# Clustered attention and two MLP layers on one core: inverse sums spread by transposes, a mask transposed by pairs of tiles, the first MLP weights decoded in a written order

## The chip, the core and the metric

The kernel runs on one core of one Trainium2 chip. The metric is device time in microseconds (us), from the start of the program to its end; before the change it is 804.18 us, the median of three runs. The engines are named as the profile names them: PE (TensorE; its weight loads are PEld), DVE (VectorE), ACT (ScalarE), POOL (GpSimd) and SP (SyncE, which issues the DMAs). Each takes its instructions in the order of its own queue, and waits for others by semaphores.

## What is computed

Attention over 2 batches of 8 heads, 768 rows, head size 64, in which a query sees only the keys of its own cluster of 16; the result is the input of two MLP layers one after the other (512 to 2048 to 512, on 1536 tokens).

```python
    q_assign = np.argmax(np.einsum('bhsd,hcd->bhsc', q_n, c_n), axis=-1)
    k_assign = np.argmax(np.einsum('bhsd,hcd->bhsc', k_n, c_n), axis=-1)
    mask = q_assign[:, :, :, None] == k_assign[:, :, None, :]
    scores = scale * np.matmul(q, k.transpose(0, 1, 3, 2))
    scores = np.where(mask, scores, -1000000000.0)
    scores = scores - np.max(scores, axis=-1, keepdims=True)
    attn = np.exp(scores)
    attn = attn / (np.sum(attn, axis=-1, keepdims=True) + 1e-09)
    return np.matmul(attn, v).astype(np.float32)
...
    h = np.maximum(x @ w_in, 0.0)
    return (h * h @ w_out).astype(np.float32)
...
    h = x @ w_in
    relu6 = np.clip(h + 3.0, 0.0, 6.0)
    g = h * relu6 / 6.0
    return (g @ w_out).astype(np.float32)
```

Here `q_n`, `k_n` and `c_n` are the rows of q, k and the centroids divided by their norms. The inputs come as 64-bit floats in HBM: the weights are read as pairs of 32-bit words and put together on the chip ("decoding").

## The kernel before

**Precision.** Every fp32 operand of a product is split in two parts (`H` and `L`, `eh` and `el`, `gh` and `gl`, `xh` and `xl`, `hi` and `lo` of `w`) that PE multiplies at its faster rate; a product is then two or three matmuls.

**Attention, to about 278 us.** A unit is two heads of one batch: 8 units, each of 12 tiles of 128 queries, 96 tiles in all. A tile `n` goes through these steps: four matmuls `s` (L650 the products, L653 with the 16 mask rows behind a part of the operand `op`), the row maximum on DVE (L659), the exponential and its row sum on ACT (L670), two groups of three transposes on PE (L686), the split into `eh` and `el`, and the matmuls with the values (L713, four in a tile). The split is done by ACT and DVE, or, for the places in the set `ON_POOL` (11 of the 24 in a unit), by a copy `et` to SBUF and two POOL operations (L178, L694). `schedule` writes the order out by hand: each tile has five slots, and the tables `STEPS`, `FIRST`, `WEIGHTS`, `EARLY` and `AV` name the tile, relative to a unit's first, and the slot at which each other step of the unit is put: loads of the next unit's q, k and v, their transposes `tq` (L401), 12 stacking DMAs of 192 KB into `op`, cluster similarities, the mask, and after the unit the normalisation. POOL, DVE, ACT and PE get their instructions in that order; SP the DMAs.

**The mask.** `onehot` makes `oh`, 128 rows by 6 tiles by 64 columns (4 heads' worth of cluster flags for q and k). `mask` transposes each of the six on PE into one PSUM tile `toh` (L511), and one ACT operation over 64 partitions and 768 columns scales it into `mt` (L516), which four small DMAs (L524) bring into the rows 64 to 80 of `op`.

**The normalisation.** The 12 row sums of a unit are inverted on DVE into `ri`, 128 queries by 12. `emit_rows` transposes `ri` (`tr`, L742), splits it in `rh` (ACT, L745) and `rl` (DVE, L746), and sends the parts with four DMAs (L750) into four spare partitions, 96 to 99, of the next unit's `op` tile. `emit_norm` spreads them over 128 partitions by one matmul with a matrix `spread` of ones (`tn`, L759, twice a unit), multiplies the unnormalised result `U_t` by it on DVE, and splits into `XH`, `XL` on POOL. The last unit has no next `op` tile: there ACT writes a copy `rb` of `ri`, each value 64 times (L767), and three transposes of 128 by 128 (L769) bring it into place.

**The MLP, from about 278 us.** `decode` turns a chunk of weights (128 by 512 values, 512 KB in HBM) into `hi` and `lo` by seven steps: a clamp on POOL (`t`, L191), a scaling on ACT (`u`, L196), three integer operations on DVE (L201, L203, L208), a rounding on ACT (`hi`, L212) and a difference on DVE (`lo`, L214). Four chunks make one block of `w_in` or `w_out`. The first block of `w_in` is decoded in halves during the attention (`WEIGHTS`), as are the first 384 tokens' hidden values (`emit_early`). `mm1` makes the hidden values of a group of tokens, 4 `fb` of 12 matmuls, each `fb` followed by `gate` (ACT, ACT, POOL, DVE); `mm2` multiplies them by a block of `w_out`, 4 `db` of 12 matmuls, each with all four chunks. For the first block the tokens go in four groups of 384, after that in three of 512. This stage isn't written out by hand: a scheduler orders it from the program, whose loop asks for `mm1` of the groups 1 and 2, then `mm2` of 0 and 1, and so on, and whose tiles `t`, `u` and `a` of the decoding (`wd`) have one buffer each.

Of the kernel before, what the change touches and what calls it, by code (L numbers as in the profile page):

```python
# [23 lines left out]
    "load q": (-19, 0),  # L24
    "load k": (-24, 2),
    "load v": (-12, 4),
    "q0": (-15, 3),
    "q1": (-14, 1),
    "k0": (-14, 3),
    "k1": (-12, 0),  # L30
    "stack0": (-8, 3),
    "sim0": (-12, 4),
    "sim1": (-10, 0),
    "assign": (-10, 4),
    "stack1": (-6, 2),
    "leader": (-10, 4),
    "onehot": (-6, 2),
    "mask": (-5, 4),
    "v0": (-5, 2),
    "v1": (-3, 4),  # L40
    "rinv": (11, 0),
    "rows": (12, 2),
    "norm0": (16, 1),
    "norm1": (17, 0),
# [5 lines left out]
        "second1": (0, 3),  # L50
        "mask": (2, 1),
        "v0": (1, 3),
        "v1": (2, 3),
# [3 lines left out]
        "load v": (-7, 1),  # L57
        "k0": (-12, 1),
        "k1": (-10, 2),
        "stack0": (-10, 2),  # L60
        "sim0": (-9, 4),
        "sim1": (-7, 2),
        "assign": (-6, 2),
        "stack1": (-9, 0),
        "leader": (-6, 2),
        "onehot": (-5, 2),
        "mask": (-4, 3),
        "v0": (-2, 3),
        "v1": (0, 0),
    },  # L70
    2: {
        "load q": (-18, 4),
        "load k": (-17, 1),
        "load v": (-10, 3),
# [5 lines left out]
WEIGHTS = ((0, 2), (3, 4), (4, 4), (6, 0), (6, 3), (7, 3), (9, 3), (10, 0))  # L80
WEIGHTS_7 = (
    ((-1, 3), (0, 0), (0, 4), (1, 1), (1, 3), (1, 4), (2, 0), (2, 0)),
    ((2, 0), (4, 4), (5, 0), (5, 0), (5, 2), (5, 4), (6, 2), (7, 2)),
# [6 lines left out]
    ((2, 1), (2, 4), (3, 1)),  # L90
    ((5, 3), (5, 4), (6, 1)),
    ((7, 1), (7, 4), (9, 0)),
    ((9, 1), (10, 1), (10, 4)),
)

AV = ((3, 3), (3, 4), (4, 4), (5, 0), (5, 2), (5, 2))
# [3 lines left out]
    (0, 0), (1, 0), (1, 1), (2, 1), (4, 0), (4, 1), (6, 0), (7, 0), (9, 0), (9, 1), (11, 1),  # L100
# [5 lines left out]
    (0, 0), (2, 0), (4, 0), (5, 0), (6, 1), (8, 0), (8, 1), (9, 0), (10, 0),  # L106
# [4 lines left out]
    (2, 0), (5, 0), (6, 1), (10, 0),  # L111
# [6 lines left out]
E_U = "v"  # L118
# [3 lines left out]
E_XL = "p"  # L122
BIG = float(2**60)
# [5 lines left out]
def cluster_attention_mlp_kernel(  # L129
# [50 lines left out]
    def decode(pool, hi, lo, r, on_dve, clamp_on_dve=False):  # L180
# [7 lines left out]
        t = pool.tile(sh, F32, tag="t", name="t")  # L188
        u = pool.tile(sh, F32, tag="u", name="u")
        a = pool.tile(sh, I32, tag="a", name="a")  # L190
# [6 lines left out]
        else:  # L197
            nc.vector.tensor_scalar(u, t, 2.0**-112, None, op0=ALU.mult)
        yield
        ui = u.bitcast(I32)  # L200
        nc.vector.tensor_scalar(a, ui, 3, None, op0=ALU.logical_shift_left)  # L201
# [5 lines left out]
        v = t.bitcast(I32)  # L207
        nc.vector.scalar_tensor_tensor(  # L208
            v, ui, -0x80000000, a, op0=ALU.bitwise_and, op1=ALU.bitwise_or
# [40 lines left out]
    with ExitStack() as actx:  # L250
# [5 lines left out]
        msc = ac.tile([64, 1], F32, name="msc")  # L256
        mbi = ac.tile([64, 1], F32, name="mbi")
        nc.vector.memset(msc[0:32], 1.0)
        nc.vector.memset(msc[32:64], BIG)
        nc.vector.memset(mbi[0:32], 0.0)  # L260
        nc.vector.memset(mbi[32:64], -BIG)
        C = ac.tile([P, NJ, 160], F32R, name="c")
        C0 = ac.tile([P, 160], F32R, name="c0")
        spread = ac.tile([P, P], F32R, name="spread")[96:100]
# [76 lines left out]
        def centroid_prep(c):  # L341
# [4 lines left out]
            ones = sm_p.tile([P, HS], F32, tag="xx", name="ones")[96:100, :P]  # L346
            ones = ones.rearrange("p (i d) -> p i d", i=2)
            nc.gpsimd.memset(ones, 1.0)
            for base, sign in ((0, 1), (1, -1)):
                nc.gpsimd.affine_select(  # L350
                    ones, ones, pattern=[[-2 * sign, 2], [0, D]], compare_op=ALU.is_ge, fill=0.0,
                    base=base, channel_multiplier=sign,
                )
# [3 lines left out]
            nc.vector.tensor_copy(spread, ones.rearrange("p i d -> p (i d)"))  # L357
# [19 lines left out]
        def prep(u):  # L377
# [129 lines left out]
            def mask(r0=0, r1=R):  # L507
# [6 lines left out]
                if r0 == 0:  # L514
                    st["m"] = pr_p.tile([64, S], F32, tag="sim", name="mt", bufs=1)
                nc.scalar.activation(  # L516
                    st["m"].bitcast(F32R)[0:64, r0 * P : r1 * P], t[0:64, :n], AF.Identity,
                    scale=msc, bias=mbi,
                )
# [76 lines left out]
            def second_head(n):  # L596
# [27 lines left out]
                "rows": lambda: emit_rows(u),  # L624
# [112 lines left out]
        def emit_rows(u):  # L737

            if u == NU - 1:
                return  # L740
            t = ps_t.tile([P, 512], F32, tag="t", name="tr")
            nc.tensor.transpose(t[0 : 2 * R, :P], rinv[u], ident)  # L742
            rh = sm_p.tile([2 * R, P], F32R, tag="rh", name="rh", bufs=1)
            rl = sm_p.tile([2 * R, P], F32R, tag="rl", name="rl", bufs=1)
            nc.scalar.activation(rh, t[0 : 2 * R, :P], AF.Copy)  # L745
            nc.vector.tensor_sub(rl, t[0 : 2 * R, :P], f(rh))  # L746
            rows[u] = oper[u + 1][1][96:100, 1]
# [122 lines left out]
    with ExitStack() as mctx:  # L870
# [96 lines left out]
        for s, (m, fq, c, n) in enumerate(steps):  # L967
# [7 lines left out]
            if s:  # L975
                mm1(m, fq, c, n)
# [39 lines left out]
```

## Time and profile before

| | us |
|---|---|
| three runs | 801.37, 804.18, 806.17 |
| the profiled execution, its own time | 805.96 |
| its span (first to last instruction) | 804.3 |
| PE busy | 784.9 (98%) |
| DVE busy | 531.7 (66%) |
| ACT busy | 396.6 (49%) |
| POOL busy | 324.9 (40%) |
| mean granted clock of PE | 0.995 |

Busy is time in which an engine works on an instruction; matmuls overlap, so that a busy PE may still advance at less than its pace. For PE the time from one row's start to the next row's start tells more than a row's duration. A row on a stretch gives the busy times of PE, PEld, DVE, ACT and POOL in this order. A timeline row is: start, duration, engine, line, operation, output and inputs with their shapes, how many follow one another, and in brackets how long the engine had been idle before and what ended that.

### The profile page before, as it was taken

The numbers are of one execution on the slowest core, as the hardware profiler recorded it, in microseconds if no ns is written. First come the engines' busy times: TensorE is split into PE (matmuls) and PEld (weight loads), VectorE is DVE, ScalarE is ACT, GpSimd is POOL, SyncE is SP. The second block draws the span as 40 slices with busy tenths as digits, with TensorE's granted clock in tenths as the row PEclk, the third lists the DMA queues.
The fourth block names the chain that finished last, engine by engine and source line by source line (L and its number), as shares of the span: only waits on it lengthen the run. The fifth ranks groups of instructions, "written<-read, shape, count | busy, mean of one in ns | idle before, by whom it ended". The sixth has DMA issues, their size and how long they took to land.

```text
span 804.3 us, 11576 instructions
## 1 busy us (share of the span) xinstructions
PE 784.9 (98%) x4069; PEld 676.4 (84%) x4069; DVE 531.7 (66%) x897; ACT 396.6 (49%) x794; POOL 324.9 (40%) x441
## 2 busy tenths in 40 slices
PE   7989999999999989999999999999999999999998
PEld 6878998888888879988888888888888888888887
DVE  6879889888898574666666456586555665733432
ACT  5888898888886554554434334332343232211110
POOL 1759788778794551222322222333222222211110
PEclk9999999999999998999999999999999999999999
DMA  8838539448332023333222122121221211000012
GB/s 178 173 72 188 123 80 200 107 96 189 95 93 67 1 81 103 105 105 99 85 78 88 45 78 66 40 84 48 79 79 52 79 53 52 27 1 1 13 52 93
DMA packets 58537, 67.35 MB, mean 84 GB/s; under 512 B 41320, under 2 KB 41744, under 8 KB 58480
## 3 DMA queue, kind: packets, MB, share of 16 engines
q1 hardware_dynamic: 58480, 66.62, 31.2%
q8 instruction: 32, 0.52, 0.3%
q14 instruction: 25, 0.20, 0.1%
HBM read 43.02 MB, written 3.15 MB: 57 GB/s over the span
## 4 chain that ended last, share of the span: by engine, by line
PE 82%; DVE 4%; DMA 4%; ACT 3%; POOL 3%; issue 2%; SPq 2%; ACTq 0%; DVEq 0%; POOLq 0%
PE o L937 33%; PE h L231 30%; PE a L713 6%; PE t L686 5%; DMA op<-HL 3%; PE s L650 3%; PE s L653 2%; PE tsim L446 1%; SPq L298 1%; DVE nm L659 1%; POOL el L694 1%; ACT et L175 1%; DVE el L697 1%; DMA op<-mt 1%; PE tq L401 1%
## 5 line engine op out<-in xcount | busy, mean ns | idle before, releaser
L231 PE MATMUL h<-xh,w 128*128 128x512 f32 (+1 forms) x800 | 245.3, 382 | 0.5 <-ACT et L175 0.5
L231 PEld LDWEIGHTS h<-xh,w 128*128 128x128 f32 x800 | 149.3, 188 | 27.0 <-ACT et L175 0.7
L231 PE MATMUL h<-xl,w 128*128 128x512 f32 (+1 forms) x400 | 152.3, 381 | 0.0
L178 POOL TENSOR_SCALAR gh<-g 128x512 fp32r<-128x512 f32 (+1 forms) x96 | 70.5, 734 | 193.9 <-DVE g L242 133.5
L937 PE MATMUL o<-w,gh 128*128 128x512 f32 (+1 forms) x392 | 120.4, 385 | 0.0
L937 PE MATMUL o<-gh,w 128*128 128x512 f32 (+1 forms) x384 | 115.2, 376 | 0.0
L191 POOL TENSOR_SCALAR t<-wr 128x512 f32<-128x512 f32 (+1 forms) x66 | 46.4, 703 | 163.4 <-DVE w L214 162.2
L212 ACT ACTIVATE w<-t 128x512 fp32r<-128x512 f32 (+1 forms) x68 | 41.3, 607 | 127.3 <-DVE t L208 89.3
L244 DVE TENSOR_TENSOR gl<-g,gh 128x512 fp32r<-128x512 f32 (+1 forms) x96 | 65.2, 680 | 54.5 <-POOL gh L178 54.5
L686 PE MATMUL t<-ident,e 128*128 128x128 f32 x576 | 93.7, 275 | 4.5 <-ACT e L670 3.6
L659 DVE TENSOR_REDUCE nm<-s 128x1 f32<-128x768 f32 x96 | 91.0, 948 | 5.5 <-PE s L653 4.7
L694 POOL TENSOR_TENSOR el<-et,eh 128x384 fp32r<-128x384 f32 x86 | 89.1, 1036 | 7.2
L670 ACT ACTIVATE e<-s,nm 128x768 f32<-128x768 f32 x96 | 86.4, 900 | 3.0 <-DVE nm L659 2.7
L231 PEld LDWEIGHTS h<-xl,w 128*128 128x128 f32 x400 | 75.1, 188 | 13.0
L686 PEld LDWEIGHTS t<-ident,e 128*128 128x128 f32 x576 | 70.4, 140 | 17.9 <-ACT e L670 7.2
L937 PEld LDWEIGHTS o<-w,gh 128*128 128x128 f32 x392 | 73.1, 188 | 14.6
L937 PEld LDWEIGHTS o<-gh,w 128*128 128x128 f32 x384 | 71.4, 188 | 11.6 <-issue 0.3
L241 ACT ACTIVATE r<-h,three 128x512 f32<-128x512 f32 x48 | 32.5, 682 | 90.2 <-PE h L231 90.2
L196 ACT ACTIVATE u<-t 128x512 f32<-128x512 f32 (+1 forms) x62 | 38.7, 625 | 77.5 <-POOL t L191 76.5
L937 PE MATMUL o<-w,gl 128*128 128x512 f32 (+1 forms) x196 | 75.4, 385 | 0.0
L713 PE MATMUL a<-eh,vs 128*128 128x384 f32 x192 | 71.2, 371 | 1.2 <-DVE u L727 1.2
L937 PE MATMUL o<-gl,w 128*128 128x512 f32 (+1 forms) x192 | 72.1, 376 | 0.0
(127 smaller groups left out, 1273.8 us busy)
## 6 DMA issues: line engine op xcount, KB each, us to landing
wr<-in_moe_w_out_dram SPq DMA_DIRECT2D x32, 512.0 KB
op<-HL SPq DMA_DIRECT2D x84, 192.0 KB
wr<-in_moe_w_in_dram SPq DMA_DIRECT2D x28, 512.0 KB
rawv<-in_v_dram SPq DMA_DIRECT2D x16, 192.0 KB
out_dram<-acc SPq DMA_DIRECT2D x11, 256.0 KB
rawq<-in_q_dram SPq DMA_DIRECT2D x14, 192.0 KB
rawk<-in_k_dram SPq DMA_DIRECT2D x14, 192.0 KB
wr<-in_moe_w_in_dram SPq DMA_DIRECT2D x8, 256.0 KB
```

Source lines behind the costliest of these rows:

```text
L178: nc.gpsimd.tensor_scalar(dst, src, 1.0, 0.0, op0=ALU.mult, op1=ALU.add)
L191: (nc.vector if clamp_on_dve or not on_dve and E_CLAMP == "v" else nc.gpsimd).tensor_scalar(t, f(hw), MOST, -MOST, op0=ALU.min, op1=ALU.max)
L196: nc.scalar.activation(u, t, AF.Copy, scale=2.0**-112)
L212: nc.scalar.activation(hi, t, AF.Copy)
L231: nc.tensor.matmul(h, w[:, d, fs], x[:, d, cs], start=(d == 0 and n == 0), stop=(d == ND - 1 and n == 2),)
L244: nc.vector.tensor_sub(gl, g, f(gh))
L659: nc.vector.tensor_reduce(nm, S_t[n][:, :, :HS], axis=AX.XY, op=ALU.max, negate=True)
L670: nc.scalar.activation(e, s[:, :, :HS], AF.Exp, bias=nm, accum_out=sums[u][:, i * R + r : i * R + r + 1])
L686: nc.tensor.transpose(t[:, c, :], E_t[n][:, half, c * P : (c + 1) * P], ident)
L694: nc.gpsimd.tensor_sub(el, et, f(eh))
L713: nc.tensor.matmul(a[:, :HS], vs[:, kr, i, :], x[:, kr, :], start=(kr == 0 and x is eh), stop=(kr == R - 1 and x is el),)
L937: nc.tensor.matmul(o, lhsT, rhs, start=(k == 0), stop=(k == 3 * NF - 1))
```

## The change

- **Normalisation.** `emit_rows`, its transpose, its two operations and its four DMAs go, and so does `spread`. For every unit a copy `rb` (128 by 384, each inverse 64 times) is made twice, on POOL for the first seven units, on ACT for the last, at two new slots `spread0` and `spread1`; `emit_norm` transposes it in three pieces for all units.
- **Mask.** Two tiles of `oh` (128 columns) go through one transpose: three in place of six; the result lies in two halves of the partitions, so ACT scales it with two operations of 64 by 384.
- **Decoding.** The tile `a` goes, the integer steps work in `u` and `t`. In the weights decoded during the attention, `u` is made on ACT in place of DVE.
- **Begin of the MLP.** `mm1` of groups 1, 2 and 3 and `mm2` of groups 0, 1 and 2 are written out by hand, with the steps of the eight chunks of the next two blocks put between them by `decoding`; `t` has three buffers, `u` two; group 3's hidden values have a pool of their own. The weight pools are taken before the others, so their first buffers lie where the attention's tiles lay.
- **Slots.** Nearly all numbers of the tables are new; `ON_POOL` has ten places in place of eleven, `ON_POOL_LAST` ten in place of nine.

```diff
-    "mask": (-5, 4),
+    "mask": (-6, 3),
...
     "rinv": (11, 0),
-    "rows": (12, 2),
-    "norm0": (16, 1),
+    "rinv": (11, 3),
+    "spread0": (13, 1),
+    "spread1": (14, 1),
...
-E_U = "v"
+E_U = "a"
+E_RB = "p"
...
-        a = pool.tile(sh, I32, tag="a", name="a")
...
-                n = (r1 - r0) * P
-                for r in range(r0, r1):
+                for c in range(3):
                     nc.tensor.transpose(
-                        t[0:64, (r - r0) * P : (r - r0 + 1) * P], st["oh"][:, r, :], identb
+                        t[:, c * P : (c + 1) * P],
+                        st["oh"][:, 2 * c : 2 * c + 2, :].rearrange("p r c -> p (r c)"), identb,
                     )
...
+                for h in range(2):
+                    rs = slice(64 * h, 64 * h + 64)
+                    nc.scalar.activation(
+                        m[:, h], t[rs, : 3 * P].rearrange("p (c q) -> p c q", q=P), AF.Identity,
+                        scale=msc[rs], bias=mbi[rs],
+                    )
...
-        def emit_rows(u):
...
-            nc.tensor.transpose(t[0 : 2 * R, :P], rinv[u], ident)
...
-            nc.scalar.activation(rh, t[0 : 2 * R, :P], AF.Copy)
-            nc.vector.tensor_sub(rl, t[0 : 2 * R, :P], f(rh))
...
-                    nc.sync.dma_start(
-                        f(rows[u])[2 * i + x : 2 * i + x + 1, :],
...
+        def emit_spread(u, half):
...
+            rb = sm_p.tile([P, HS], F32, tag="rb", name="rb")
...
+            src = rinv[u].rearrange("p (i h r) -> p h r i", i=2, h=2)[:, half]
+            src = src.unsqueeze(3).to_broadcast([P, 3, 2, D])
+            if E_RB == "a" or u == NU - 1:
+                nc.scalar.activation(rb, src, AF.Copy)
+            else:
+                nc.gpsimd.tensor_copy(rb, src)
...
-                nc.tensor.matmul(
-                    t[:, :HS], spread, rows[u][:, half * HS : half * HS + HS], start=True, stop=True
+            for c in range(3):
+                nc.tensor.transpose(
+                    t[:, c * P : (c + 1) * P], rb[:, c].rearrange("p i d -> p (i d)"), ident
                 )
...
+        wd_p = mctx.enter_context(tc.tile_pool(name="wd", bufs=2, reuse_waits="tile"))
-        wd_p = mctx.enter_context(tc.tile_pool(name="wd", bufs=1, reuse_waits="tile"))
...
+        with tc.manual_schedule():
+            chunks = load_w(0, 0, 1) + load_w(0, 1, 0)
+            pieces = [2]
+            run(chunks[0], 2)
...
+            def decoding(after):
...
+                c, odd = divmod(pieces[0], 2)
+                pieces[0] += after
+                for when, chunk, n in (
+                    ((0, 0), c - 1, 3), ((0, 1), c - 2, 1), ((0, 1), c, 1),
+                    ((1, 1), c - 2, 2), ((1, 1), c, 1),
+                ):
+                    if when == (odd, after) and 0 <= chunk < len(chunks):
+                        run(chunks[chunk], n)
...
+            for step in steps[1:4]:
+                mm1(*step, decoding)
+            for n, step in enumerate(steps[:3]):
+                mm2(*step, decoding)
```

**Where the instructions stand.** PE, in a middle unit where the first half of the unit before is normalised, before the change (`a` values matmuls, `t` transposes of `e`, `s` scores):

```order
L686 MATMUL t<-ident,e 128x128 [waits DVE_49,PE_49,Activation_49]
L686 MATMUL t<-ident,e 128x128 x2
L759 MATMUL tn<-op,spread 128x384 [waits DMAHW5_49,DMAHW4_49,DMAHW6_49,DMAHW3_49,DVE_49]
L650 MATMUL s<-op 128x384 x2
L653 MATMUL s<-op 128x384 [waits DMAHW2_49,DMAHW1_49]
```

And the same place after it:

```order
L682 MATMUL t<-ident,e 128x128 [waits DVE_49,PE_49,Activation_49]
L682 MATMUL t<-ident,e 128x128 x2
L750 MATMUL tn<-ident,rb 128x128 [waits DVE_49,Pool_49]
L750 MATMUL tn<-ident,rb 128x128 x2
L646 MATMUL s<-op 128x384 [waits DMAHW6_49,DMAHW5_49]
```

One matmul that waited for four DMAs has become three transposes that wait for POOL's copy; the transpose `tr`, which stood some four tiles earlier, has gone.

SP's queue between two units, before: the mask's rows, then the inverses' rows, then the loads of the unit after the next and the first stacking DMAs.

```order
L524 DMA op<-mt 16x768 x4
L750 DMA op<-rh 1x6x128
L750 DMA op<-rl 1x6x128
L750 DMA op<-rh 1x6x128
L750 DMA op<-rl 1x6x128
L298 DMA rawk<-in_k_dram 128x6x64 x2
L324 DMA wr_823<-in_moe_w_in_dram 128x512
L298 DMA rawv<-in_v_dram 128x6x64 x2
```

After:

```order
L418 DMA op<-HL 64x768
L419 DMA op<-HL 64x768
L420 DMA op<-HL 64x768
L519 DMA op<-mt 16x768 x4
L325 DMA wr_1212<-in_moe_w_in_dram 128x512
L299 DMA rawv<-in_v_dram 128x6x64 x2
L299 DMA rawk<-in_k_dram 128x6x64 x2
L299 DMA rawq<-in_q_dram 128x6x64 x2
```

Behind the mask's rows SP now has the loads at once; the q load has come to them from behind the first stacking DMAs.

DVE at the begin of the MLP, one and a half chunks before the change (L201 to L208 the integer steps, L214 `lo`, L244 the gate's `gl`):

```order
L201 TENSOR_SCALAR a<-u 128x512 [waits Activation_49]
L203 SCALAR_TENSOR_TENSOR a<-wr,a 128x512 [waits DMAHW2_49,DVE_49]
L208 SCALAR_TENSOR_TENSOR t<-u,a 128x512 [waits DVE_49]
L244 TENSOR_TENSOR gl<-g,gh 128x384 [waits Pool_49]
L214 TENSOR_TENSOR w<-t,w 128x512 [waits Activation_49]
L201 TENSOR_SCALAR a<-u 128x512 [waits Activation_49]
```

And after:

```order
L205 SCALAR_TENSOR_TENSOR u<-wr,u 128x512 [waits DMAHW5_49,DVE_49]
L209 SCALAR_TENSOR_TENSOR t<-t,u 128x512 [waits DVE_49]
L245 TENSOR_TENSOR gl<-g,gh 128x384 [waits Pool_49] x2
L215 TENSOR_TENSOR w<-t,w 128x512
L203 TENSOR_SCALAR u<-u 128x512 [waits Activation_49]
L205 SCALAR_TENSOR_TENSOR u<-wr,u 128x512 [waits DMAHW6_49,DVE_49]
```

Two `gl` now stand ahead of each `lo`, which no longer waits for ACT by itself, and the next chunk's clamp has its own buffer `t`. On PE 144 matmuls of `mm1` now stand ahead of the first `mm2`, where 96 stood.

## Rows read from the trace of the kernel before

**Rows 1.** Stretches: from:to, us, each engine's busy time (instructions), PEclk, DMA share, GB/s

```profile
82.80:113.70 30.90, 30.67 (x205) 27.78 (x204) 27.69 (x49) 27.01 (x62) 25.41 (x33) 1.00 0.61 131
144.80:176.90 32.10, 31.05 (x205) 27.62 (x203) 27.43 (x49) 26.93 (x61) 25.37 (x33) 1.00 0.57 127
...
301.60:321.70 20.10, 19.67 (x96) 19.41 (x96) 8.77 (x15) 8.47 (x18) 2.58 (x4) 0.83 0.32 103
321.70:341.80 20.10, 20.10 (x109) 18.97 (x109) 12.27 (x21) 10.30 (x20) 5.03 (x8) 1.00 0.32 105
```

**Rows 2.** Timeline of PE at the begin of the MLP

```profile
294.45 1.20 PE L937 MATMUL o<-g,w 128*128 128x384 f32 x6
296.75 2.73 PE L937 MATMUL o<-g,w 128*128 128x384 f32 x12 [1.10 <-ACT w L212]
302.03 8.33 PE L937 MATMUL o<-g,w 128*128 128x384 f32 x30 [2.54 <-ACT w L212]
310.19 0.34 PE L231 MATMUL h<-xh,w 128*128 128x384 f32 x1
...
311.02 0.41 PE L937 MATMUL o<-gh,w 128*128 128x384 f32 x1
...
319.45 0.33 PE L231 MATMUL h<-xl,w 128*128 128x384 f32 x1
```

**Rows 3.** Timeline of POOL there, and all `lo` operations of DVE (shortest/median/longest ns)

```profile
286.61 1.01 POOL L191 TENSOR_SCALAR t<-wr 128x512 f32<-128x512 f32 x1
...
292.25 0.64 POOL L191 TENSOR_SCALAR t<-wr 128x512 f32<-128x512 f32 x1 [2.01 <-DVE w L214]
...
L214 DVE TENSOR_TENSOR w<-t,w x62: 415/693/1504, 244.5 to 699.3; 128x512 fp32r<-128x512 f32 x60, 128x256 fp32r<-128x256 f32 x2
```

**Rows 4.** Timeline of PE about `tn` and `tr`, and the last unit's transposes `tn`

```profile
124.42 0.49 PE L686 MATMUL t<-ident,e 128*128 128x128 f32 x3
124.84 0.44 PE L759 MATMUL tn<-op,spread 4*128 4x384 f32 x1
125.21 0.62 PE L650 MATMUL s<-op 128*128 128x384 f32 x2
125.67 0.52 PE L653 MATMUL s<-op 80*128 80x384 f32 x2
126.02 0.49 PE L686 MATMUL t<-ident,e 128*128 128x128 f32 x3
126.27 0.42 PE L713 MATMUL a<-eh,vs 128*128 128x384 f32 x1
...
177.59 0.51 PE L653 MATMUL s<-op 80*128 80x384 f32 x2
...
178.28 0.55 PE L686 MATMUL t<-ident,e 128*128 128x128 f32 x3
...
279.66 0.55 PE L769 MATMUL tn<-ident,rb 128*128 128x128 f32 x3
279.97 0.42 PE L231 MATMUL h<-xl,w 128*128 128x384 f32 x1
```

**Rows 5.** Timeline of PE about the six transposes `toh` of the mask

```profile
132.96 0.49 PE L686 MATMUL t<-ident,e 128*128 128x128 f32 x3
133.38 0.52 PE L511 MATMUL toh<-identb,oh 128*64 128x128 bf16 x6
133.84 0.44 PE L713 MATMUL a<-eh,vs 128*128 128x384 f32 x1
```

**Rows 6.** Groups: line, engine, op, tiles, count, busy us, mean ns, idle before

```profile
L694 POOL TENSOR_TENSOR el<-et,eh 128x384 fp32r<-128x384 f32 x86 | 89.1, 1036 | 7.2
...
L767 ACT ACTIVATE rb<-ri 128x384 f32<-128x384 f32 x2 | 1.0, 518 | 0.2 <-PE tn L769 0.2
```

**Rows 7.** Waits of SP's queue (us in total, times, longest), and a wait of PE

```profile
SPq L750 <- ACT eh L696: 52.3, 6, 9.5
...
47.86 0.61 PE L653 MATMUL s<-op 80*128 80x384 f32 x2 [1.07 <-DMA op<-mt]
```

More of the change, by code (lines that the diff above doesn't have):

```diff
@@ L49 @@
         "second0": (0, 0),
[L50 to L53, printed above, removed]
+        "second1": (1, 0),
+        "mask": (2, 0),
+        "v0": (2, 1),
+        "v1": (2, 2),
     },
@@ L56 @@
         "q1": (-12, 0),
[L57 to L69, printed above, removed]
-    },
-    2: {
-        "load q": (-18, 4),
-        "load k": (-17, 1),
-        "load v": (-10, 3),
+        "load v": (-6, 4),
+        "k0": (-11, 4),
+        "k1": (-10, 3),
+        "stack0": (-9, 1),
+        "sim0": (-8, 0),
+        "sim1": (-7, 1),
+        "assign": (-7, 3),
+        "stack1": (-9, 1),
+        "leader": (-6, 0),
+        "onehot": (-5, 0),
+        "mask": (-4, 0),
+        "v0": (-3, 3),
+        "v1": (1, 0),
+    },
+    2: {
+        "load q": (-18, 1),
+        "load k": (-18, 3),
+        "load v": (-10, 2),
     },
@@ L110 @@
 ET_DVE_LAST = {
[L111 removed]
+    (2, 0), (7, 1),
 }
@@ L122 @@
 E_XL = "p"
+E_RB = "p"
+DEC = 4
 BIG = float(2**60)
@@ L755, in emit_norm @@
         def emit_norm(u, half):
             b, j = units[u]
+            rb = rows.pop((u, half))
             t = ps_t.tile([P, 512], F32, tag="t", name="tn")
[L758 to L771 removed]
+            for c in range(3):
+                nc.tensor.transpose(
+                    t[:, c * P : (c + 1) * P], rb[:, c].rearrange("p i d -> p (i d)"), ident
+                )
@@ L889, in load_w, with chunk, run @@
             idx[0] += 1
-            hi, lo = w[:, 0], w[:, 1]
-            for c in range(4):
+            wts[m, fq, which] = (w[:, 0], w[:, 1])
+            def chunk(c):
                 r = wr_p.tile([P, 512, 2], I32, tag="wr", name="wr")
                 nc.sync.dma_start(r.rearrange("p f w -> p (f w)"), src[:, c])
-                for _ in decode(wd_p, hi[:, c], lo[:, c], r, True):
-                    pass
-            wts[m, fq, which] = (hi, lo)
+                yield from decode(wd_p, w[:, 0, c], w[:, 1, c], r, True, bufs=3)
+            return [chunk(c) for c in range(4)]
+        def run(steps, n=None):
+            for _ in range(n) if n else iter(int, 1):
+                if next(steps, 0) == 0:
+                    break
         acc = acc_p.tile([P, 4, NT], F32, name="acc")
@@ L901, in cluster_attention_mlp_kernel, with mm1 @@
         G = {(0, 0, 0): early[0]}
-        def mm1(m, fq, c0, n):
+        def mm1(m, fq, c0, n, between=None):
             wh, wl = wts[m, fq, 0]
-            gh = g_p.tile([P, NF, TC], F32R, tag="gh", name="gh")[:, :, :n]
-            gl = g_p.tile([P, NF, TC], F32R, tag="gl", name="gl")[:, :, :n]
+            if (m, fq, c0 + n) == (0, 0, NT):
+                gh, gl = (g3_p.tile([P, NF, n], F32R, tag=x, name=x) for x in ("gh3", "gl3"))
+            else:
+                gh = g_p.tile([P, NF, TC], F32R, tag="gh", name="gh")[:, :, :n]
+                gl = g_p.tile([P, NF, TC], F32R, tag="gl", name="gl")[:, :, :n]
             for fb in range(NF):
@@ L913, in mm1, with mm2 @@
                 gate(m, h, r, g, gh[:, fb], gl[:, fb])
+                if between:
+                    between(1)
             G[m, fq, c0] = (gh, gl)
-        def mm2(m, fq, c0, n):
+        def mm2(m, fq, c0, n, between=None):
             wh, wl = wts[m, fq, 1]
@@ L951, in mm2 @@
                         nc.vector.tensor_tensor(a, a, o, op=ALU.add)
+                    if between:
+                        between(0)
+                        between(1)
                     if last and m == 0:
@@ L965, in cluster_attention_mlp_kernel @@
                 steps += [(m, fq, c, n) for c in range(0, NT, n)]
-        load_w(0, 0, 1)
+        with tc.manual_schedule():
[15 more added lines that the diff above has]
+                mm2(*step, decoding)
+        for chunk in load_w(0, 1, 1):
+            run(chunk)
         for s, (m, fq, c, n) in enumerate(steps):
+            if s < 4:
+                continue
             if c == 0:
@@ L970, in cluster_attention_mlp_kernel @@
                 if nx[0] < 2:
-                    load_w(*nx, 0)
-                    load_w(*nx, 1)
-            if s:
-                mm1(m, fq, c, n)
-            if s == 2:
-                mm2(*steps[0])
-            if s > 1:
-                mm2(*steps[s - 1])
+                    for chunk in load_w(*nx, 0) + load_w(*nx, 1):
+                        run(chunk)
+            mm1(m, fq, c, n)
+            mm2(*steps[s - 1])
         mm2(*steps[-1])
```

127 lines of the change are left out of this document (49 added, 78 removed).

## The prediction, made before the changed kernel was run

> **What bounds the kernel now.** I read the stretches first, to see which engine has no time left in which stage; then the timeline of PE where the stages meet; then the rows about the operations that the diff takes away; last the waits. In the MLP PE has no gap: 20.10 us busy of 20.10, while DVE stands at 12.27 [rows 1]. The change doesn't alter the products of that stage, so nothing is to be had there beyond its begin. In a middle unit of the attention PE is busy 30.67 of 30.90 us, DVE 27.69, ACT 27.01, POOL 25.41 [rows 1]: PE is the bound, but DVE is at 90% and ACT at 87%. One unit took 32.10 us with the same work, 1.2 us more than its neighbour. Where the stages meet the granted clock falls to 0.83 as the mean of 20.1 us, the only stretch of the four that isn't at 1.00 [rows 1]; there PE waits twice for the first block of `w_out` [rows 2].
>
> So three places can give time: the meeting of the stages, PE's own work in the attention, and waits for DMAs in the attention.
>
> **The change part by part.** First, *the begin of the MLP*. The first `mm2` is 48 matmuls (6, 12 and 30 in the rows), from 294.45 to 310.19 us: 15.74 us [rows 2]. The next `mm2`, 48 matmuls of the same shape, goes from 311.02 to 319.45: 8.43 us [rows 2]. The difference, 7.3 us, is in two parts: idle stretches of 1.10 and 2.54 us and those at reduced pace, for the 30 matmuls after the longer wait take 8.16 us, 272 ns each, against 176 ns in the undisturbed block. The row of the stretch shows the clock down after these waits; 1.2 GHz, half of 2.4 GHz, is the lower of its two levels, and 0.83 is the mean of both over that stretch.
>
> What was waited for is `hi` of the chunks. The clamps of two chunks that follow each other start at 286.61 and 292.25, 5.64 us apart, and POOL sat idle 2.01 us before the second until DVE's `lo` of the chunk before was done [rows 3]: with one buffer of `t` the chunks go one at a time. Now `t` has three buffers, chunk 0 is loaded and clamped before the last tile's values are multiplied, and 144 matmuls stand ahead of the first `mm2` in place of 96. At 8.43 us for 48 these are 25.3 us. At the old rhythm the last of four chunks begins 16.9 us after the first and takes another 5.6: 22.5 us, inside the 25.3 even if the new buffers gained nothing. I therefore count the whole 7.3 us as gone. The weights behind it, the second block of `w_in`, get three `mm1` and three `mm2`, 50 us, for eight chunks; at 5.64 us each these are 45. Nothing of the decoding is added, so no engine is asked for more; only the order differs.
>
> Chunk 0's load lands in space of the attention's `op` tiles and so waits for the last scores; its clamp stands in POOL's queue ahead of the last tile's `eh` and `el`, which PE's last values matmuls wait for. I count this at nothing: before those matmuls PE has a dozen `mm1` matmuls (about 2 us) to do. Without that cover it costs the clamp's 1.01 us [rows 3], once.
>
> Second, *PE's work in the attention*. `tr`: the scores' last pair to the next transposes takes 0.69 us with it (177.59 to 178.28) and 0.35 without it (125.67 to 126.02) [rows 4], 0.34 for each of seven units: 2.4 us gone. `tn`: from transposes to the next work is 0.79 us with it (124.42 to 125.21) and 0.25 without (126.02 to 126.27) [rows 4], so 0.54; fourteen are 7.6 us. In their place come fourteen times three transposes, as the last unit has them: 0.31 (279.66 to 279.97) [rows 4], 4.3 us. Net 3.2 gone. Mask: from transposes to values is 0.88 us with the six in between (132.96 to 133.84) [rows 5], 0.63 above the 0.25; eight are 5.0. Three of 128 columns, taken at 0.31, are 2.5. Net 2.5. Together 8.1 us, about one in each unit.
>
> PE can only go as fast as its feeders. DVE loses `rl` and a 256-wide scaling for each half block of weights and gets one more `el`; ACT loses `rh`, gets that scaling and cuts the mask operation in two: both come out within a few tenths of a microsecond in a unit, each piece is of the size of ACT's 128 by 384 copy, 518 ns [rows 6], or smaller. Their 27.69 and 27.01 us would then stand against 29.9 in place of 30.9 us, 93 and 90%. POOL loses one `eh` and `el` (1.04 us the second) [rows 6] and gets two copies `rb`. The trace has no such copy on POOL; ACT's takes 518 ns and POOL's two-input operation of that size 1036 [rows 6], so two cost 1.0 to 2.1 us and POOL's load hardly moves. No row shows PE fed at 93%, so between all of the 8.1 us and none I take two thirds, nearer to all since no engine's load grows: 5.4 us.
>
> Third, *DMAs*. SP's queue waited 52.3 us in six stretches for the inverses' `rh`, up to 9.5 us [rows 7], with the loads and the stacking of the next units queued behind. Those four DMAs go, and nothing takes their place. Most of these waits were hidden; the late unit's 1.2 us [rows 1] and the 1.07 us that PE waited for the mask's rows [rows 7] are what shows, 2.3 together. The second lies in the first units, where loads come thick; I take 1.0 of 2.3, with 0 and 2.3 as ends.
>
> The centroids' preparation and the smaller slot moves I count at nothing; they lie beside PE's work, and each is shorter than a microsecond.
>
> **The sum.** 7.3 + 5.4 + 1.0 = 13.7 us, made against the profiled execution's own 805.96: 792.3. That execution lies 1.8 us above the median of the runs, 804.18, so the forecast is 790.5 us.
>
> **The rivals.** *Feeders bind.* PE's shorter work in the attention gives nothing because DVE and ACT, at 90 and 87%, or the order of a queue, already set the pace. For it: 8% is not much slack for engines in fixed order. Against it: PE shows 0.23 us idle in a unit. Then only the MLP's 7.3 us are left: 796.9 us. Chance 0.15.
>
> *The decoding still comes late.* The written order interleaves DVE's five steps with `gl`, while POOL works. One `lo` took 1504 ns where the median is 693 [rows 3], beside POOL at work. If each DVE step of the four chunks were stretched like that one, by 2.2 times, a chunk would need more than the 6.6 us that 25.3 us leave it, and the wait would stay: 13.7 less 7.3 is 6.4, 797.8 us. Against it: one stretched `lo` in a chunk still gave the 5.64 us rhythm. Chance 0.08. The Trainium skill, "GPSIMD Engine Reference", § 8 Key points, says that GpSimd shares its SBUF interfaces with VectorE and contends with DVE instructions that read two SBUF inputs, as `lo` does; by that rule alone the wait would stay wherever POOL is busy all along. The trace agrees in the longest `lo`, 1504 ns, not in the median, 693.
>
> *POOL's copies on the path (slower).* `rb` is queued on POOL ahead of the `eh` and `el` for which PE's values matmuls wait, and PE's `tn` itself now waits for it. Where POOL is just in time, PE loses the length of each copy. Fourteen copies outweigh the 13.7 us and the 4 us of what can be told apart only above 1.27 us each, more than POOL's slowest row of that size, 1036 ns [rows 6], and only if none is hidden. At one and a half times that row, 1.55 us, all exposed, they cost 21.8: 8.1 slower, 812.3 us. Chance 0.05: reading each value 64 times is the one thing that no POOL row shows.
>
> *It doesn't do what it says.* PE's order at the meeting stays bound by something that the rows don't name, and new slots take back what the transposes give: 804 us. Chance 0.05.
>
> *More than forecast.* All of the 8.1 and 2.3 us come: 17.7, 786.5 us or less. Chance 0.07.
>
> **How the numbers follow.** The forecast has 0.60. The range takes in 786.5 and 797.8, and at both ends the 1 to 2 us by which runs of one kernel differ: 784 to 799 us. I call half a per cent, 4 us, about what a measurement can tell from no change: faster than 800.2 are the forecast, the faster case and most of the two at 797 and 798, 0.87; slower than 808.2 the copies, 0.05; the rest, 0.08, lies between.
>
> **What would show it.** At the meeting PE's 48 first `mm2` matmuls should take about 8.4 us, with no wait for ACT and the clock at 1.00 in every stretch; from 144 `mm1` matmuls to `mm2` there should be no gap. A middle unit should take 30.2 us or less, with PE as busy as before; if it stays at 30.8 with PE idle before transposes or values, the feeders bind. SP should have no long wait between a unit's mask and the next loads. POOL's `rb` should last 0.5 to 1.04 us, with no wait of `tn` or of the values behind it. I am wrong if PE waits for `w` at the first `mm2`, if a unit is no shorter, or if `rb` lasts much above a microsecond.

## The result: 790.74 us

The changed kernel took 790.74 us in the median of four runs (789.97 to 791.11), the kernel before 803.35 us beside it (801.37 to 806.17). The ratio is 0.984, 95% interval 0.981 to 0.987. The prediction was 790.5 us.

Stretches of the profiled execution after the change (790.8 us, span 789.0 us; columns as in [rows 1]): a middle unit, the attention's end, and the begin of the MLP.

```profile
81.40:111.50 30.10, 29.47 (x206) 27.95 (x205) 27.88 (x48) 27.66 (x63) 24.52 (x33) 1.00 0.61 134
264.00:272.00 8.00, 6.85 (x44) 6.49 (x43) 4.20 (x10) 4.29 (x11) 3.05 (x4) 1.00 0.23 71
272.00:292.00 20.00, 20.00 (x117) 20.00 (x116) 14.89 (x23) 12.66 (x26) 12.69 (x17) 1.00 0.26 78
292.00:312.00 20.00, 19.87 (x113) 19.12 (x111) 17.06 (x26) 11.48 (x24) 7.59 (x9) 1.00 0.41 126
```

The unit takes 30.10 us where the row before says 30.90 [rows 1], and the clock is at 1.00 throughout; the stretch at 0.83 is gone. PE's busy time in a unit fell by 1.2 us (30.67 to 29.47), but PE, idle 0.23 us of a unit before, is now idle 0.63. The timeline of PE after shows this gap, the last matmuls of the attention, and the first `mm2`:

```profile
101.83 0.55 PE L682 MATMUL t<-ident,e 128*128 128x128 f32 x3 [0.63 <-ACT e L666]
...
268.96 0.41 PE L709 MATMUL a<-eh,vs 128*128 128x384 f32 x1 [1.15 <-DVE u L723]
...
294.34 8.93 PE L933 MATMUL o<-g,w 128*128 128x384 f32 x48
303.11 0.39 PE L232 MATMUL h<-xh,w 128*128 128x512 f32 x1
```

The first `mm2` now takes 8.77 us (294.34 to 303.11) in place of 15.74 [rows 2], 7.0 less. The gap before the transposes in each middle unit is new. It ends with the exponential, and the timeline of ACT after shows what stood ahead of that:

```profile
98.53 0.49 ACT L692 ACTIVATE eh<-t 128x384 fp32r<-128x384 f32 x1
98.90 1.34 ACT L511 ACTIVATE mt<-toh,mbi,msc 64x384 fp32r<-64x384 bf16 x2
100.26 0.49 ACT L178 ACTIVATE et<-t 128x384 f32<-128x384 f32 x1
100.78 0.90 ACT L666 ACTIVATE e<-s,nm 128x768 f32<-128x768 f32 x1
```

These are the mask's two operations, 1.34 us in a row. Two groups after the change, and the waits of SP's queue (total, times, longest):

```profile
L742 POOL COPY rb<-ri 128x384 f32<-128x384 f32 x14 | 7.0, 503 | 0.0
L511 ACT ACTIVATE mt<-toh,mbi,msc 64x384 fp32r<-64x384 bf16 x16 | 10.6, 665 | 0.7 <-PE toh L503 0.5
...
SPq L299 <- POOL vs L535: 36.6, 5, 7.4
SPq L519 <- ACT et L178: 25.8, 6, 5.5
```

POOL's copy takes 503 ns, and no row shows PE's `tn` waiting for it. SP's wait for the inverses, 52.3 us [rows 7], has gone, but SP waits no less, now for the buffer of v and for the mask: 62.4 us in the two rows. PE's own waits for DMAs, 1.07 us at one place before [rows 7], are no longer among the waits of over half a microsecond.

### The profile page after: what moved, and what is told of

Same layout as the page of the kernel before. It is cut to its first block, busy times and chain, and to the rows that moved or that the text cites. A ratio compares the mean times of both kernels' runs of the same rounds, so it can differ in the third digit from the quotient of the medians.

```text
span 789.0 us, 11571 instructions
## 1 busy us (share of the span) xinstructions
PE 771.8 (98%) x4066; PEld 674.8 (86%) x4066; DVE 547.9 (69%) x891; ACT 399.7 (51%) x803; POOL 328.5 (42%) x440
## 4 chain that ended last, share of the span: by engine, by line
PE 85%; ACT 5%; DVE 5%; issue 2%; POOL 2%; DMA 1%; SPq 0%; ACTq 0%; POOLq 0%
PE o L933 33%; PE h L232 29%; PE a L709 6%; PE t L682 6%; PE s L646 3%; PE s L649 3%; ACT e L666 2%; PE tsim L438 2%; PE tq L393 1%; ACT mt L511 1%; DVE nm L655 1%; ACT eh L692 1%; DVE el L693 1%; ACT et L178 1%; ACT tmp L178 1%
## 5 line engine op out<-in xcount | busy, mean ns | idle before, releaser
L181 POOL TENSOR_SCALAR gh<-g 128x512 fp32r<-128x512 f32 (+1 forms) x96 | 68.9, 718 | 228.1 <-DVE g L243 150.0
L245 DVE TENSOR_TENSOR gl<-g,gh 128x512 fp32r<-128x512 f32 (+1 forms) x96 | 70.4, 736 | 70.4 <-POOL gh L181 70.4
L193 POOL TENSOR_SCALAR t<-wr 128x512 f32<-128x512 f32 (+1 forms) x66 | 56.0, 852 | 113.2 <-DVE w L215 44.5
L690 POOL TENSOR_TENSOR el<-et,eh 128x384 fp32r<-128x384 f32 x80 | 81.8, 1023 | 6.7
L198 ACT ACTIVATE u<-t 128x512 f32<-128x512 f32 (+1 forms) x68 | 41.3, 607 | 68.4 <-POOL t L193 67.9
L213 ACT ACTIVATE w<-t 128x512 fp32r<-128x512 f32 (+1 forms) x68 | 39.3, 604 | 69.3 <-PE o L933 41.7
L693 DVE TENSOR_TENSOR el<-t,eh 128x384 fp32r<-128x384 f32 x112 | 61.4, 551 | 14.7 <-ACT eh L692 13.3
```

The source lines that it names most:

```text
L181: nc.gpsimd.tensor_scalar(dst, src, 1.0, 0.0, op0=ALU.mult, op1=ALU.add)
L193: (nc.vector if clamp_on_dve or not on_dve and E_CLAMP == "v" else nc.gpsimd).tensor_scalar(t, f(hw), MOST, -MOST, op0=ALU.min, op1=ALU.max)
L198: nc.scalar.activation(u, t, AF.Copy, scale=2.0**-112)
L245: nc.vector.tensor_sub(gl, g, f(gh))
L690: nc.gpsimd.tensor_sub(el, et, f(eh))
L693: nc.vector.tensor_sub(el, t, f(eh))
```

## The experiments

All were timed in five rounds beside the kernel before; its median in the three sessions was 804.13, 805.18 and 804.0 us. Ratios are to it, with 95% intervals; the differences to the changed kernel are of medians, against 790.74. The changed kernel was timed beside a fourth median of the kernel before, 803.35; these medians lie up to 1.8 us apart, so a difference of that size is told apart only where the traces show it too, in the length of a unit or in a wait.

### The MLP stage undone, and alone

`a_mlp_old` puts the MLP stage of the kernel before behind the changed attention.

```diff
-        with tc.manual_schedule():
...
-            for step in steps[1:4]:
-                mm1(*step, decoding)
-            for n, step in enumerate(steps[:3]):
-                mm2(*step, decoding)
...
+        load_w(0, 0, 1)
+        for s, (m, fq, c, n) in enumerate(steps):
...
+            if s == 2:
+                mm2(*steps[0])
+            if s > 1:
+                mm2(*steps[s - 1])
```

> The changed kernel, with the MLP stage of the kernel before (its loop order, the scheduler's order, one buffer for each tile of the decoding). Theory (terms add up, the meeting of the stages is worth 7.3 us): 798 us, with the first mm2's 48 matmuls at 15 to 16 us, two waits for hi on ACT and a stretch below full clock. Rival (the gain there comes mostly from the attention's end, or the wait would be gone anyway with earlier slots): under 3 us more than the changed kernel's 790.7.

Measured: 797.19 us, ratio 0.992 (0.990 to 0.993), 6.5 us more than the changed kernel. PE's timeline at the first `mm2` of `a_mlp_old`:

```profile
285.21 1.69 PE L918 MATMUL o<-g,w 128*128 128x384 f32 x7
290.83 8.96 PE L918 MATMUL o<-g,w 128*128 128x384 f32 x41 [3.92 <-ACT w L213]
299.63 0.34 PE L232 MATMUL h<-xh,w 128*128 128x384 f32 x1
```

The wait for `hi` is back, 3.92 us in one piece where two were expected, and the 48 matmuls take 14.4 us (285.21 to 299.63). The opposite experiment, `b_mlp_new`, gives the kernel before the changed MLP stage with its decoding:

> The kernel before, with the changed MLP stage alone (written order at its begin, three mm1 ahead, three buffers of t, decoding in place). Undoing the stage cost the changed kernel 6.4 us. Theory (the same gain by itself): 804 to 805 less 6 to 8, 797 to 799 us, no wait of PE for hi at the first mm2 and the full clock there. Rival (it needs the early slots of the changed attention, chunk 0 comes too late behind the attention's end): 800 us or more.

Measured: 797.37 us, ratio 0.991 (0.989 to 0.994), 6.6 us less than the kernel before, and no wait for `hi` in its trace. Undone or alone, the stage is worth about 6.5 us: the first theory.

### Is it the buffers or the order?

`a_bufs_only` is `a_mlp_old` with three buffers of `t` and two of `u`.

```diff
-                for _ in decode(wd_p, hi[:, c], lo[:, c], r, True):
+                for _ in decode(wd_p, hi[:, c], lo[:, c], r, True, bufs=3):
```

> The changed kernel with the MLP stage of the kernel before, but three buffers of t and two of u. Theory 1 (one chunk at a time was the cause): most of the 6.4 us comes back, 791 to 793 us. Theory 2 (too few mm1 ahead of the first mm2, the order is the cause): still 796 to 797.5 us, PE waiting 3 to 4 us for hi.

Measured: 796.28 us, ratio 0.990 (0.988 to 0.993): 5.5 us more than the changed kernel. The buffers alone give at most 0.9 us, less than the sessions differ by, and the waits for the weights are as long in sum, 3.93 us. PE's timeline at its first `mm2`:

```profile
284.37 1.29 PE L918 MATMUL o<-g,w 128*128 128x384 f32 x6
288.29 0.61 PE L918 MATMUL o<-g,w 128*128 128x384 f32 x2 [2.64 <-ACT w L213]
289.94 1.01 PE L918 MATMUL o<-g,w 128*128 128x384 f32 x2 [1.03 <-DVE w L215]
291.20 9.16 PE L918 MATMUL o<-g,w 128*128 128x384 f32 x38 [0.26 <-ACT w L213]
```

So the second theory: 96 matmuls ahead, in the scheduler's order, are too few. `a_auto_1buf` has the other half: three `mm1` ahead, but one buffer, and the scheduler's order.

```diff
-            for step in steps[1:4]:
-                mm1(*step, decoding)
-            for n, step in enumerate(steps[:3]):
-                mm2(*step, decoding)
+        for chunk in load_w(0, 0, 1) + load_w(0, 1, 0):
+            run(chunk)
+        for step in steps[1:4]:
+            mm1(*step)
+        for step in steps[:3]:
+            mm2(*step)
```

> The changed kernel with one buffer of t and u, no written order in the MLP (the scheduler's), but three mm1 ahead of the first mm2. The prediction's working says that at the old rhythm of 5.64 us a chunk four chunks need 22.5 us, less than the 25.3 us of three mm1, so the buffers are not needed. Theory (that holds): 790.5 to 792 us, no wait for hi above 0.3 us. Rival (the chunks start later than counted, or the old rhythm stretches with the gates between): 793 to 797 us with a wait at the first mm2.

Measured: 800.34 us, ratio 0.995 (0.993 to 0.997), 9.6 us more than the changed kernel and worse than the stage of before. Neither expectation named what happened. PE's timeline, one row of POOL's, and ACT's:

```profile
294.61 8.48 PE L933 MATMUL o<-g,w 128*128 128x384 f32 x48
...
311.52 0.69 PE L933 MATMUL o<-gh,w 128*128 128x384 f32 x1 [7.74 <-ACT acc L941]
...
309.79 0.63 POOL L193 TENSOR_SCALAR t<-wr 128x512 f32<-128x512 f32 x1 [4.12 <-DVE w L215]
...
308.36 0.63 ACT L213 ACTIVATE w<-t 128x512 fp32r<-128x512 f32 x1 [2.02 <-DVE t L209]
310.46 0.63 ACT L198 ACTIVATE u<-t 128x512 f32<-128x512 f32 x1 [1.47 <-POOL t L193]
310.99 1.62 ACT L941 ACTIVATE acc<-o 128x384 f32<-128x384 f32 x4
```

The first `mm2` does run without a wait, as the prediction's arithmetic said for the old rhythm. But then PE waits 7.74 us, because four results `acc` stand on ACT behind `u` and `hi` of the next block's chunks, which themselves wait for one another's single buffer: POOL's clamp waits for the `lo` of the chunk before (the row of POOL). So the matmuls ahead aren't enough when decoding that waits stands on ACT ahead of what PE needs. Whether three buffers or the written order alone would have mended that isn't shown, for this run has neither.

### The spreading undone, and alone

`a_rows` is the changed kernel with `emit_rows` and the spreading matmul.

```diff
-    "spread0": (13, 1),
-    "spread1": (14, 1),
+    "rows": (12, 2),
...
-            for c in range(3):
-                nc.tensor.transpose(
-                    t[:, c * P : (c + 1) * P], rb[:, c].rearrange("p i d -> p (i d)"), ident
+                nc.tensor.matmul(
+                    t[:, :HS], spread, rows[u][:, half * HS : half * HS + HS], start=True, stop=True
```

> The changed kernel, with the inverse sums spread as before: transpose tr, split, four small DMAs, one spreading matmul twice a unit; slot of the rows as before, all else as changed. Theory (PE is the bound, so PE's work counts one for one): tr 2.4 us and tn 3.2 us come back, and up to 2 us of DMA waits: 796 to 798 us, a middle unit 30.8 to 31 us. Rival (DVE and ACT set the pace): within 1 us of the changed kernel's 790.7, a unit still 30.1 us.

Measured: 799.15 us, ratio 0.994 (0.993 to 0.996), 8.4 us more than the changed kernel, above both expectations. A middle unit's stretch and PE's gaps in it:

```profile
83.10:114.30 31.20, 30.18 (x203) 27.65 (x201) 27.81 (x49) 27.79 (x64) 23.52 (x31) 1.00 0.57 129
...
84.65 0.27 PE L746 MATMUL tr<-ident,ri 128*12 128x128 f32 x1 [0.39 <-DVE ri L739]
...
104.61 0.55 PE L690 MATMUL t<-ident,e 128*128 128x128 f32 x3 [0.63 <-ACT e L674]
```

The unit is 1.1 us longer: 0.7 us more of PE's work (30.18 against 29.47) and 0.39 us in which `tr` waits for the sums' inverses, which the changed slots put later. `b_norm_new` is the kernel before with the new spreading alone:

> The kernel before, with the new spreading of the inverse sums alone (copies on POOL at tile 13 and 14, transposes), all other slots and the MLP as before. Undoing it cost the changed kernel 8.4 us. Theory (it is worth that whatever the slots): 804.1 less 7 to 9, 795 to 797 us. Prediction's own terms (2.4 and 3.2 of PE work, about 1 of waits): 797.5 us. Rival (part of the 8.4 us was that the old slot of the rows came too early behind the new slot of the sums): 798.5 to 801 us.

Measured: 798.16 us, ratio 0.991 (0.989 to 0.994), 7.0 us less than the kernel before. That is nearest to the prediction's own terms (6.6 us less), at the theory's lower end (7 to 9) and less than the 8.4 us. The last expectation named why: the waits of `tr` for the inverses, 0.39 us in six units and 0.72 in the seventh, 3.1 us in `a_rows`, are a price that the old spreading pays in the new slots only.

### The mask undone, apart, and in one operation

`a_mask6` has six transposes and one ACT operation again.

```diff
-                for c in range(3):
+                for r in range(r0, r1):
...
-                for h in range(2):
...
+                nc.scalar.activation(
+                    st["m"].bitcast(F32R)[0:64, r0 * P : r1 * P], t[0:64, :n], AF.Identity,
+                    scale=msc, bias=mbi,
+                )
```

> The changed kernel, with the mask transposed by single tiles again (six transposes, one ACT operation of 64x768). Theory (PE's work counts one for one): 2.5 us back, 793.2 us. Rival (the wait of 0.63 us that PE has in every middle unit for the exponential comes from the two mask operations of 0.67 us that stand ahead of it on ACT): one operation of 0.98 us in place of 1.33 gives 0.35 us a unit back to PE, which takes back what the transposes cost: 790 to 791.5 us.

Measured: 788.42 us (787.77 to 789.27), ratio 0.981 (0.979 to 0.983): 2.3 us *less* than the changed kernel. This part of the change costs time: from one mask to the next a middle unit takes 29.82 us here (97.47 to 127.29) and 30.07 in the changed kernel (97.85 to 127.92). In `a_mask6` PE's gap is 0.16 us and the operation is one:

```profile
101.11 0.55 PE L678 MATMUL t<-ident,e 128*128 128x128 f32 x3 [0.16 <-ACT e L662]
...
L507 ACT ACTIVATE mt<-toh,mbi,msc 64x768 fp32r<-64x768 bf16 x8 | 7.9, 984 | 0.9 <-PE toh L502 0.9
```

`a_mask_apart` keeps the change's two operations, but puts the second behind the next exponential.

```diff
+    "mask1": (-5, 2),
...
-                for h in range(2):
+            def mask_half(h):
```

> The changed kernel, but ACT's second mask operation stands behind the next exponential instead of ahead of it. Theory (the 0.63 us wait of PE for the exponential in each middle unit is the price of two mask operations in a row): the wait falls below 0.1 us in seven units, 786 to 787 us. Rival (ACT or DVE have no room anywhere, the wait only moves; or the mask's DMAs come late): 789.5 to 792 us, with waits of the same size at another place of the unit.

Measured: 790.75 us (790.55 to 791.65), ratio 0.984 (0.982 to 0.986), no change. PE's gap for the exponential fell to 0.32 us, but a unit is as long as before; the rival held, and the wait moved: the transposes at 99.92 come 0.48 us behind the scores ahead of them, where 0.35 is usual, and those at 100.81 come 0.32 behind values matmuls, where 0.18 is. These, and the gap that is left:

```profile
99.44 0.52 PE L657 MATMUL s<-op 80*128 80x384 f32 x2
99.92 0.55 PE L690 MATMUL t<-ident,e 128*128 128x128 f32 x3
...
100.49 0.34 PE L717 MATMUL a<-el,vs 128*128 128x384 f32 x1
100.81 0.55 PE L690 MATMUL t<-ident,e 128*128 128x128 f32 x3
...
103.41 0.55 PE L690 MATMUL t<-ident,e 128*128 128x128 f32 x3 [0.32 <-ACT e L674]
```

`a_mask_one` keeps the three transposes and does both halves in one operation over 128 partitions; the mask's rows then take eight small DMAs.

```diff
-                for h in range(2):
...
+                nc.scalar.activation(
+                    st["m"].bitcast(F32R), t[:, : 3 * P], AF.Identity, scale=msc, bias=mbi
+                )
...
+                for h in range(2):
+                    m = st["m"][64 * h + row : 64 * h + row + NCL]
+                    nc.sync.dma_start(o[:, h], m.rearrange("p (c q) -> p c q", q=P))
```

> The changed kernel with three transposes of the mask as changed, but one ACT operation over all 128 partitions and 384 columns, and eight small DMAs of the mask's rows in place of four. Theory (PE's three transposes saved count, and ACT's work ahead of the exponential sets the wait): the two operations cost 665 ns each, one of the same width should too, 0.33 us less than the single 64x768 one, so the best of both: 785.5 to 787.5 us. Rival (four more DMAs on SP bring the mask late): 789 us or more, with PE waiting for mt.

Measured: 787.48 us (787.18 to 787.88), ratio 0.978 (0.976 to 0.981), the fastest kernel here, 3.3 us under the changed one. The stretch of a middle unit and the operation:

```profile
80.40:110.00 29.60, 29.44 (x206) 28.01 (x205) 28.06 (x48) 26.96 (x62) 24.58 (x33) 1.00 0.60 137
...
L508 ACT ACTIVATE mt<-toh,mbi,msc 128x384 fp32r<-128x384 bf16 x8 | 5.4, 679 | 0.5 <-PE toh L503 0.5
```

The unit is 29.6 us, half a microsecond less than in the changed kernel, with PE idle 0.16. The rival, DMAs too late, shows only outside the middle units: PE waits 1.5 us once for the mask's rows in the first units.

### How full ACT and DVE are

`a_u_dve` and `a_rb_act` each change one letter.

```diff
-E_U = "a"
+E_U = "v"
...
-E_RB = "p"
+E_RB = "a"
```

> The changed kernel, with u of the weights decoded during the attention on DVE again. The first runs showed PE waiting for the exponential behind ACT's mask operations. Theory (ACT is the feeder that binds, at a few places in the unit): 0.41 us a unit off ACT gives up to that back where it stood ahead of an exponential, 788 to 790 us. Rival 1 (it stood where ACT waits anyway): 790.0 to 791.2 us. Rival 2 (DVE binds as much): 791.5 to 794 us.

> The changed kernel, with the copies rb on ACT (about 0.52 us each) instead of POOL (0.50 us). Theory (POOL has room for them, ACT has none): 14 copies of 0.52 us, half to all of them on PE's path: 794 to 798 us. Rival (ACT has room at these slots): 790 to 792 us. On neither is a copy longer than 0.6 us, against the rival of the prediction that needed 1.27 us.

Measured: 794.22 us with `u` on DVE, ratio 0.987 (0.984 to 0.989), 3.5 us more; 794.57 us with the copies on ACT, ratio 0.987 (0.985 to 0.989), 3.8 us more. A middle unit of each (the first with DVE at 29.04 of 30.65 us, the second with ACT at 28.51 of 30.60), with a gap that `a_u_dve` alone has, in each middle unit, and DVE ahead of it:

```profile
81.40:112.05 30.65, 29.49 (x205) 27.93 (x204) 29.04 (x49) 27.52 (x63) 24.61 (x34) 1.00 0.59 132
...
97.58 0.64 DVE L200 TENSOR_SCALAR u<-t 128x256 f32<-128x256 f32 x1
...
99.47 0.54 DVE L723 TENSOR_TENSOR u<-a,tmp 64x384 f32<-64x384 f32 x1
...
100.16 0.41 PE L709 MATMUL a<-eh,vs 128*128 128x384 f32 x1 [0.52 <-POOL xh L181]
...
130.79 0.41 PE L709 MATMUL a<-eh,vs 128*128 128x384 f32 x1 [0.52 <-POOL xh L181]
...
81.60:112.20 30.60, 29.65 (x205) 27.78 (x203) 27.88 (x48) 28.51 (x64) 23.64 (x31) 1.00 0.60 131
```

The row of the gap names POOL's `xh`, which those matmuls don't read. They do need the one buffer of `a`, which DVE's L723 frees. In `a_u_dve` that ends at 100.01, in a queue in which the scaling at 97.58 is new, 0.15 us ahead of these matmuls; in the changed kernel it ends at 98.01, 0.14 us ahead of them, and there is no gap. By these times DVE binds in the first, as rival 2 said, and the result lies just above its 794 us; in the second the theory held at its lower end: of 14 copies of 0.52 us, 7.2 us in all, half came through. Either makes a unit 0.5 to 0.6 us longer, for about 1 us more of work on DVE (27.88 to 29.04) or ACT (27.66 to 28.51), which then stand at 95 and 93% of the unit.

### All three undone

> The changed kernel with the old spreading, the old mask and the old MLP stage: what is left of the change are its slots, the places on POOL and u on ACT. If the parts undone singly add up (6.4 for the MLP, 8.4 for the spreading, the mask 2.3 the other way), it takes 790.7 + 6.4 + 8.4 - 2.3 = 803.2 us, and the slots with u on ACT are worth 1 to 2 us against the kernel before. Rival (the parts overlap, each undone alone counts what another also gives): 798 to 801 us. Rival (the new slots suit only the new operations): 805 us or more.

Measured: 801.16 us, ratio 0.996 (0.995 to 0.998), 2.8 us less than the kernel before. That is what the slots, one place fewer on POOL, `u` on ACT and the decoding without `a` give by themselves. The parts undone singly, 6.5 and 8.4 less 2.3, are 12.6 us and would give 803.3; together they cost 10.4, so that 2.2 us overlap. This lies between the first theory and the rival. How the 2.8 us divide among slots and places was not tried.

## Why the prediction came out right

**Begin of the MLP, 7.3 us: right in size, with one step of it wrong.** The first `mm2` lost 7.0 us of its length; undone and alone the stage is worth 6.5. The step counted at nothing, the last values matmuls, has a price. PE waits 1.15 us there after the change, and 0.17 to 0.19 in the kernels with the same slots whose chunk 0 isn't decoded early (`a_mlp_old`, `a_bufs_only`); with the slots of before it had waited 0.77 already. In turn the kernel before, `a_mlp_old`, and POOL and ACT of the changed kernel:

```profile
276.35 0.42 PE L713 MATMUL a<-eh,vs 128*128 128x384 f32 x1 [0.77 <-DVE u L727]
...
267.62 0.42 PE L709 MATMUL a<-eh,vs 128*128 128x384 f32 x1 [0.17 <-DVE u L723]
...
267.43 0.51 POOL L181 TENSOR_SCALAR eh<-et 128x384 fp32r<-128x384 f32 x1 [0.73 <-ACT et L178]
...
264.51 0.63 ACT L198 ACTIVATE u<-t 128x512 f32<-128x512 f32 x1 [0.46 <-POOL t L193]
```

The dozen `mm1` matmuls didn't hide it. The price, 1.0 us, is the bound that the text gave for the cover gone, but by another path, so that the equal size is luck: POOL was idle 0.73 us before the last tile's `eh`, and what came late was ACT, on which `u` of chunk 0, itself waiting for the clamp, stands ahead of the last tile's copies. "Even if the new buffers gained nothing" was right for the first `mm2` and is open for the stage: with one buffer, in the scheduler's order, a wait of 7.74 us came behind it.

**PE's work in the attention, 8.1 us, two thirds kept: right in sum, wrong inside.** `tr` and `tn` were put at 5.6 us and brought 7.0 alone. The mask was put at 2.5 and cost 2.3. PE's own saving there did come, if smaller: from the transposes to the values it is 0.63 us after the change, where it was 0.88 [rows 5], so 0.25 a unit, 2.0 in eight.

```profile
97.52 0.49 PE L682 MATMUL t<-ident,e 128*128 128x128 f32 x3
97.85 0.33 PE L503 MATMUL toh<-identb,oh 128*128 128x128 bf16 x3
98.15 0.41 PE L709 MATMUL a<-eh,vs 128*128 128x384 f32 x1
```

The step that failed is "both come out within a few tenths of a microsecond": the cut of ACT's operation was not priced. Two of 665 ns take 0.35 us more than one of 985, and at their slot they stand ahead of an exponential: PE's gap there is 0.63 us with two operations and 0.16 with one. That takes back 0.47 us for the 0.25 saved. The feeders did bind, as the first rival said, but at single places: in `a_mask6` and `a_mask_one` less work on ACT ahead of one exponential shortens the unit, in `a_u_dve` and `a_rb_act` about 1 us more on DVE or ACT lengthens it by half as much.

**`u` on ACT and the slots, counted within tenths or at nothing:** `u` undone costs 3.5 us. The move was needed because DVE, with one more `el`, would have been at 95%. What is left of the change without its three parts is worth 2.8 us, which the sum doesn't have.

**DMA waits, 1.0 of 2.3 us: read from one execution, and the cause not borne out.** The 32.10 us unit [rows 1] and PE's wait at 47.86 [rows 7] are gone from the changed kernel: middle units are 30.1 us, all alike. But `b_mlp_new` keeps the slots and the four DMAs of before, and SP waits in it as long for the inverses' rows; yet the unit that was late is 30.77 us in its trace, and PE's wait for the mask's rows 0.21. `b_norm_new`, without those DMAs, still has 0.96 of that wait (the last row):

```profile
SPq L748 <- ACT eh L694: 51.6, 6, 9.1
...
162.26:193.03 30.77, 30.64 (x204) 27.76 (x204) 27.70 (x49) 26.91 (x62) 25.41 (x34) 1.00 0.58 130
...
46.06 0.62 PE L651 MATMUL s<-op 80*128 80x384 f32 x2 [0.21 <-DMA op<-mt]
...
47.67 0.62 PE L646 MATMUL s<-op 80*128 80x384 f32 x2 [0.96 <-DMA op<-mt]
```

So the waits don't follow from SP's queue alone, and SP's own didn't shrink. Why they come in one execution and not in another stays open.

**POOL's copies:** 503 ns, the lower bound, and no row shows PE waiting for one; the slower rival fell.

**The last subtraction was an error that others cancelled; the hit to 0.2 us is luck.** The terms were 13.7 us against an execution of 805.96; the profiled executions differ by 15.2 us, the medians by 12.6. I took 1.8 us off the result because that execution lay above its median. After the change it lies at its median (790.8 and 790.74), so the offset should not have been carried over. The third term took its waits from that same execution, so it may count as gained what the offset counts as chance. With 15.2 us the sum would have been right without the subtraction.

**A slip in the second rival:** a quarter of 25.3 us is 6.3 us for a chunk, not 6.6. Nothing else hangs on it.

## What to carry to other kernels

Where one engine is full and two others stand at 90%, price a removed instruction by what it lets the full engine skip, and every instruction put on the others by what it stands in front of: halving an operation's width didn't halve its time. A decoding that runs beside matmuls needs matmuls enough ahead of its first use *and* a place in each engine's queue behind what PE needs next; more buffers alone gained next to nothing here, and matmuls ahead alone lost time. A wait that one execution shows is a gain to count only if another execution shows it too. Undo each part of a change singly, since one of several parts may cost what the others bring.

## What the runs showed of the hardware

ACT's mask operation takes 985 ns for 64 partitions and 768 columns (the kernel before), 665 for 64 and 384 (the changed kernel), and 679 for 128 and 384 (`a_mask_one`): half the columns save a third, and twice the partitions cost 14 ns. The difference is 0.83 ns a column, which by an estimate from these two widths leaves some 0.35 us that doesn't depend on the width. POOL copies a value that it reads 64 times over, 128 by 384, in 503 ns, no slower than its other operation of this size with one input, 527 in the kernel before and 533 in the changed one.

The changed kernel's four runs lie within 1.2 us, those of the kernel before within 6.2 in its longest session (801.6 to 807.8). Both `b_mlp_new` (795.2 to 798.5) and `b_norm_new` (795.9 to 799.4) spread by over 3 us, so it isn't the meeting of the stages alone that made the times differ. The DMA waits above, over 2 us in the profiled execution before and 0.21 in that of `b_mlp_new`, are likely a part of it; why they differ was not found.
